# A spectral gate and a GEGLU layer, forward and backward: the inverse transform moves from pass one to pass two, in six classes of d mod 6

## The chip, the cores and the metric

One Trainium2 chip, one core of it. The time is device microseconds of one execution; lower is better. The engines are TensorE (PE, matmuls; PEld are its weight loads), VectorE (DVE), ScalarE (ACT), GpSimd (POOL) and SyncE (SP, which here issues most DMAs). Each engine executes its own instructions in the order in which the program lists them, and waits on semaphores for the others. In the profile, SPq and ACTq are the DMA issues in the instruction streams of SP and ACT.

## The reference

Two branches over x (2048 x 576, bf16) are mixed by a gate, and everything is differentiated by the gradient of the output:

```
g   = sigmoid((x * gate_w).sum(-1))                # one number per row
X   = rfft2(x) * (w_r + 1j * w_i)                  # 2048 x 289
a   = irfft2(X)                                    # spectral branch
b   = (gelu(B_x @ w_gate) * (B_x @ w_up)) @ w_down # F = 4608
out = g * a + (1 - g) * b
outputs: out, and the gradients to A_x, A_w_r, A_w_i, w_gate, w_up, w_down, gate_w
```

B_x enters as the same array x (`x = A_x` in the reference). The gradient to x through the spectral branch, dxa, is a second transform pair: the transform of the output's gradient (scaled by g), times the conjugate weights, transformed back. So there are two forward and two inverse 2-D transforms, of length S = 2048 along rows and D = 576 along columns.

## The kernel before

The kernel has a pass one and a pass two. The order of every engine's work is the order in which the Python code calls the instructions (a manual schedule); nothing reorders it.

**Pass one** walks over 18 groups g of 256 hidden columns, and in each over 4 pairs m of row blocks: 72 steps `pr`. A step makes the hidden activations and their gradients for 512 rows (`H_mm`, `H_act`, `H_ew1`, `H_ew2`), stores them to DRAM (`scr`), and executes the weight-gradient matmuls of the group before (`W_units`: dwd for w_down, dw for w_gate and w_up). Between these, `fft_next` drops the units of the transforms, spread evenly over the steps by `want(pr)`. In order: 32 + 32 forward units (`u1`, `u2`, along D and then the first part of S); table units (`tail_table`, `turned`); `mid` (`s2`: second part of the forward transform along S; products with the weights on DVE; `fold`; `s1`: first part of the inverse transform along S, stored to `scr_p1` and `scr_p2`); and at the end the inverse units of `inv_units`, once for a and once for dxa:

- `z(p)`: 8 matmuls of 128 columns (L888), the second part of the inverse along S for two of the 16 row classes, with the tables RT; evacuated by ACT, or by DVE in one place (L891);
- `ztail(p)`: 2 matmuls of 128 columns for the 68 columns left over (L901);
- `d(i)`: 6 matmuls for one row class (L915 with 145 columns, L917 with 290), the inverse along D; ACT or DVE evacuates (L923, L925), DVE adds and subtracts the halves (L926, L927), and SP stores the rows to `a_scr` or `dxa_scr`.

The halves come from `fold` (L810), which adds and subtracts the columns l and 288 - l before `s1`.

**Pass two** reads the stored activations back with transposing DMAs (`pin`, 144 of them, each 12 blocks of 128 x 128, six held ahead by `ensure`) and runs `jobs`: b (t) makes 128 rows of b with w_down; g (t) and u (t) make the two halves of the gradient to x with w_gate and w_up. One f0 step of a job is two `block`s of 12 matmuls of 288 columns (L1276), one for each half of the 576 columns. At jobs 1 to 9 `load_wuT` also loads a part of w_up, transposed. `post(t)` loads rows of a and of the output's gradient, and DVE makes the output and the gate's gradient; `x_end(t)` loads rows of dxa and finishes the gradient to x. PSUM has eight banks (`pacc`), handed out in pairs by `acc_pair`.

**Memory.** Two stacks of tiles grow from the two ends of the on-chip memory. `wstack` holds what pass one alone needs; it is closed before pass two's pools (p2f, p2bo, p2b, p2s, p2res) are opened, and these take the same addresses from the bottom up. A tile that lies where an earlier one lay waits for the last reader of that one. xn (all of x, 18,432 bytes in each partition) lies in `res`, which lasts to the end; dB is the first tile of `wstack`.

Of the kernel before, what the change touches and what calls it, by code (L numbers as in the profile page):

```python
# [10 lines left out]
ALU = mybir.AluOpType  # L11
# [14 lines left out]
D4NEW = 64  # L26
L2NEW = 95
# [13 lines left out]
HF = 145  # L41
QF = 73
NL = 2 * (HF - P)
# [21 lines left out]
def iotas(nc, res, unit):  # L65
# [9 lines left out]
    tb.lrow = unit([HF], F32, name="lrow")  # L75
    G.iota(tb.lrow[:], pattern=[[1, HF]], base=0, channel_multiplier=0, **kw)
    tb.dcol = res.tile([P, 8], F32, name="dcol")
# [3 lines left out]
    G.iota(tb.dcol[:, 5:7], pattern=[[1, 2]], base=0, channel_multiplier=2, **kw)  # L81
    G.iota(tb.dcol[:, 7:8], pattern=[[0, 1]], base=257, channel_multiplier=2, **kw)
    G.iota(tb.dcol[32:64, 7:8], pattern=[[0, 1]], base=256, channel_multiplier=2, **kw)
    tb.dn = res.tile([P, 8], F32, name="dn")
# [7 lines left out]
def iotas_R(nc, tb, res, unit):  # L92
# [12 lines left out]
    G.iota(tb.scol[:], pattern=[[1, T]], base=0, channel_multiplier=16, **kw)  # L105
    par_i = res.tile([P, 1], I32, name="par_i")
# [4 lines left out]
    def parity():  # L111
        V.tensor_single_scalar(par_i[:], tb.qcol_i[:], 1, op=ALU.bitwise_and)
        V.tensor_copy(tb.par[:, 1:2], par_i[:])
        V.tensor_scalar(tb.par[:, 0:1], tb.par[:, 1:2], -1.0, 1.0, op0=ALU.mult, op1=ALU.add)
        V.tensor_scalar(tb.kadd[:, 0, 1:2], tb.par[:, 1:2], float(S // 2), float(S // 4), op0=ALU.mult, op1=ALU.add)
        V.tensor_single_scalar(r4_i[:], tb.qcol_i[:], 3, op=ALU.bitwise_and)
        V.tensor_copy(tb.r4[:, 4:5], r4_i[:])
        for r in range(4):
            G.tensor_scalar(tb.r4[:, r:r + 1], tb.r4[:, 4:5], float(r), None, op0=ALU.is_equal)
# [8 lines left out]
def build_D(nc, tb, unit, c0, n, w):  # L128
# [11 lines left out]
    if c0 > 4:  # L140
        for c in range(n):
            G.tensor_scalar(X[:, c, :], tb.lrow[:, 0:w], tb.dcol[:, c0 + c:c0 + c + 1], None, op0=ALU.mult)
        G.tensor_tensor(X[:], X[:], y[:], op=ALU.add)

    def angles():
        for c in range(n if c0 <= 4 else 0):
            V.scalar_tensor_tensor(X[:, c, :], tb.lrow[:, 0:w], tb.dcol[:, c0 + c:c0 + c + 1], y[:, c, :],
                                   op0=ALU.mult, op1=ALU.add)
        V.scalar_tensor_tensor(y[:], X[:], -1.0, X[:], op0=ALU.mult, op1=ALU.max)

    def sines():
# [10 lines left out]
        elif c0 > 4:  # L162
            tb.Dt = [o[:, c] for c in range(n)]
# [10 lines left out]
    return angles, sines, tails  # L174

# [100 lines left out]
def kernel(  # L276
# [25 lines left out]
    a_scr = dram.tile([S, D], BF16, name="a_scr")  # L302
    dxa_scr = dram.tile([S, D], BF16, name="dxa_scr")
    scr_x = dram.tile([P, T, 2, DF], BF16, name="scr_x")
    scr_g = dram.tile([P, T, 2, DF], BF16, name="scr_g")
    scr_p1 = dram.tile([32, P, 2 * HF], BF16, name="scr_p1")
    scr_p2 = dram.tile([32, P, 2 * HF], BF16, name="scr_p2")

    xn = res.tile([P, T, D], BF16, name="xn")
# [5 lines left out]
    dOT = hres.tile([P, 5, T, P], BF16, name="dOT")  # L315
    dB = wstack.enter_context(tc.tile_pool(name="pdB", bufs=1)).tile([P, T, D], BF16, name="dB")
# [65 lines left out]
    tb.At2 = hres.tile([P, 2, 2, HF], BF16, name="At2")  # L382
    tb.Oi = hres.tile([P, 2, HF], BF16, name="Oi")
# [241 lines left out]
    def fwd_units(src, dst, scale, ps=pftile):  # L625
# [19 lines left out]
        def u2(t):  # L645
            def f():
# [13 lines left out]
                up = Vt[:, :, 0:2 * (HF - 1)].rearrange("p c (k l) -> p k c l", k=2)[:, :, :, 0:QF]  # L660
# [7 lines left out]
    def tail_table():  # L668

        n = HF - P  # L670
        nc.gpsimd.memset(tb.At2[:], 0.0)
        tp_ = pz.tile([P, 2, 1024], BF16, tag="z", name="tp")
        for k, r in ((2, P), (3, 32)):
            o = 512 * (k - 2)
            for c in range(2):
                nc.tensor.transpose(tp_[:, c, o:o + r], tb.Dt[k - 1][0:r, c, 0:P], ident[0:r, 0:r])
            for c in range(2):
                nc.tensor.transpose(tp_[0:n, c, o + 256:o + 256 + r], tb.Dt[k - 1][0:r, c, P:HF], ident[0:r, 0:r])
        nc.scalar.copy(tb.Oi[:, :, 0:P], tp_[:, :, 0:P])
        nc.scalar.copy(tb.Oi[:, :, P:HF], tp_[:, :, 512:512 + n])  # L680
        ot = unit([2, HF], name="ot")
        nc.scalar.copy(ot[0:n, :, 0:P], tp_[0:n, :, 256:256 + P])
        nc.scalar.copy(ot[0:n, :, P:HF], tp_[0:n, :, 768:768 + n])
        for c in range(2):
            for e, sb in enumerate((tb.Dt[2][32:64], ot)):
                r0 = 2 * n * c + (e ^ c)
                LD.dma_start(tb.At2[r0:r0 + 2 * n - 1:2, c, e, :], sb[0:n, c, :])

    tb.RT = []

    def turned(h):

        def f():
            tp_ = pftile(BF16)
            ts = range(8 * h, 8 * h + 8)
            for k, t in enumerate(ts):
                nc.tensor.transpose(tp_[:, 0, k * P:(k + 1) * P], tb.Rt[t], ident[:])
            if h == 1:
                for v in range(2):
                    nc.tensor.transpose(tp_[:, 1, v * P:(v + 1) * P], tb.B[:, v, :], ident[:])  # L700
            o = unit([8, P], name="RT")
            nc.scalar.copy(o[:].rearrange("p t m -> p (t m)"), tp_[:, 0, :])
            if h == 1:
                V.tensor_copy(tb.BT[:].rearrange("p v m -> p (v m)"), tp_[:, 1, 0:2 * P])
            tb.RT.extend(o[:, k, :] for k in range(8))
        f.room, f.last = 1.7, 2.0
        return f
# [12 lines left out]
    a_dv = a_scr[:].rearrange("(m i) d -> m i d", i=T)  # L720
    dxa_dv = dxa_scr[:].rearrange("(m i) d -> m i d", i=T)

    def mid_units():
# [40 lines left out]
        def products(p):  # L764
# [25 lines left out]
            def stack(k1, k2, conj, j):  # L790
# [9 lines left out]
                return f  # L800

            def fold(key):

                def f():
                    if key == "m1":
                        halve(st[p, "sm1"])
                    m = st[p, "s" + key][:].rearrange("p t j l -> p (t j) l")
                    q = unit([4, 2, HF], name="q" + key)
                    for e, op in enumerate((ALU.add, ALU.subtract)):
                        V.tensor_tensor(q[:, :, e, 0:HF - 1], m[:, :, 0:HF - 1], m[:, :, DF - 1:HF - 1:-1], op=op)  # L810
                    V.tensor_copy(q[:, :, :, HF - 1], m[:, :, HF - 1:HF].to_broadcast([P, 4, 2]))
                    st[p, key + "_q"] = q
                return f

            def out_dw():
# [8 lines left out]
                (0.9, lambda: (halve(G), mul("m1", X, W[:, 0])())), (0.8, mul("m2", X, W[:, 1])),  # L824
                (0.85, stack("m1", "m2", False, 0)), (0.85, stack("m1", "m2", False, 1)), (1.2, fold("m1")),
                (0.8, mul("n1", G, W[:, 0])), (0.8, mul("n2", G, W[:, 1])),
                (0.85, stack("n1", "n2", True, 0)), (0.85, stack("n1", "n2", True, 1)), (1.1, fold("n1")),
                (0.8, mul("o1", G, X[:, :, 0, :])), (0.8, mul("o2", G, X[:, :, 1, :])), (0.85, comb("o1", "o2", True)),
# [3 lines left out]
        def s1(p, key, b, dst):  # L832
            def f():
# [4 lines left out]
                q = st[p, key + "_q"][:].rearrange("p g e l -> p g (e l)")  # L838
                vps = pftile()
                for i in range(2):  # L840
                    nc.tensor.matmul(vps[:, i, :2 * HF], lhsT=tb.BT[:, int(p == 0 and b == 0 and i == 0), :], rhs=q[:, 2 * b + i, :],  # L841
                                     start=True, stop=True)
                Vt = half([2, 2 * HF], name="Vt")
                nc.scalar.copy(Vt[:].rearrange("p g (l e) -> p g e l", e=2), vps[:, :, :2 * HF].rearrange("p g (e l) -> p g e l", e=2))
# [20 lines left out]
    def inv_units(s, dv, scale):  # L865
        vp, zt = {}, {}

        def pre(i0):
            def f():
                Vp = vp[i0] = unit([2, 4 * HF], name="Vp")  # L870
                v = s[:].rearrange("g (k t c) l -> (g k) t c l", k=4, c=2)[:, i0:i0 + 2]
                LD.dma_start(Vp[:, :, 0:2 * HF], v[:, :, 0])
                LD.dma_start(Vp[:, :, 2 * HF + NL:], v[:, :, 1, 0:2 * P])
                LD.dma_start(Vp[:, :, 2 * HF:2 * HF + NL], v[:, :, 1, 2 * P:])
            f.noslot = True
            return f

        tails = {}

        def z(p):  # L880

            def f():
                Vp = vp[2 * p]
                zps = pftile()
                for ii in range(2):
                    for n in range(4):
                        c0 = (2 * HF + NL) * (n // 2) + n % 2
                        nc.tensor.matmul(zps[:, ii, n * P:(n + 1) * P], lhsT=Vp[:, ii, c0:c0 + 2 * P - 1:2],  # L888
                                         rhs=tb.RT[2 * p + ii], start=True, stop=True)
                zt[p] = unit([2, 4, P], name="ZT")  # L890
                pcopy[0](zt[p][:].rearrange("p i a m -> p i (a m)"), zps[:])  # L891
            f.wide, f.last = True, 2.0
            return f

# [531 lines left out]
```

## Time and profile before

| | us |
|---|---|
| median of three runs (lowest, highest) | 1379.36 (1379.34, 1379.62) |
| span of the profiled execution, first to last instruction | 1378.0 |
| first matmul of pass two | 949.80 |
| busy: PE, DVE, ACT, POOL | 1362.2, 789.5, 694.3, 261.9 |

The profile is one execution. Its page gives busy times, a picture of the span in 40 slices, and groups of instructions. DVE and ACT are busy in some seven to nine tenths of each slice of pass one, and in zero to six tenths of pass two:

```profile
DVE  7887777766989988876676766550002642121101
ACT  7887777767777877776766766651000000000000
```

Besides the page the trace answers questions: a timeline (start, duration, what), the list of waits (who waited for whom, in total), and busy times by stretch. A matmul's duration includes its way through the array, so matmuls that follow each other overlap in the timeline; the distance from start to start tells the rate.

### The profile page before, as it was taken

What the parts mean: (1) busy time and instruction counts of PE and PEld (TensorE: products, weight loads), DVE (VectorE), ACT (ScalarE), POOL (GpSimd) and SP (SyncE); (2) the same over time, 40 slices, a digit from 0 to 9 for tenths busy, and PEclk for the clock granted to TensorE, in tenths of its full rate; (3) what the DMA queues carried; (4) which work ended last, traced back from release to release, by engine and by line L of the source; (5) the groups of instructions that cost most, each with busy time, mean ns of one, the idle gap of its engine ahead of it and who ended that gap; (6) DMA issues with size and microseconds to landing.
All of it is one profiled execution on the core that took longest, in us unless ns stands there. A gap on an engine that the chain in (4) does not pass through costs nothing.

```text
span 1378.0 us, 25978 instructions
## 1 busy us (share of the span) xinstructions
PE 1362.2 (99%) x10186; PEld 909.0 (66%) x10272; DVE 789.5 (57%) x1526; ACT 694.3 (50%) x1288; POOL 261.9 (19%) x513
## 2 busy tenths in 40 slices
PE   9999999999999999999999999999999999999998
PEld 7566656556556556656656566556777777777776
DVE  7887777766989988876676766550002642121101
ACT  7887777767777877776766766651000000000000
POOL 6210111032444444331111011110000110000000
PEclk9999999999999999999999999999999999999999
DMA  7435444455566656555556666759999997878773
GB/s 234 126 92 150 113 124 128 129 161 154 131 163 158 169 155 168 145 144 145 144 146 163 164 163 153 180 127 280 198 192 201 218 191 169 157 161 166 156 150 88
DMA packets 512423, 218.95 MB, mean 159 GB/s; under 512 B 312010, under 2 KB 503180, under 8 KB 512300
## 3 DMA queue, kind: packets, MB, share of 16 engines
q1 hardware_dynamic: 495178, 191.89, 59.5%
q0 software_dynamic: 14912, 24.24, 6.4%
q8 instruction: 80, 1.31, 0.4%
q10 hardware_dynamic: 2210, 1.15, 0.3%
q14 instruction: 43, 0.35, 0.1%
HBM read 45.51 MB, written 98.30 MB: 104 GB/s over the span
## 4 chain that ended last, share of the span: by engine, by line
PE 96%; DVE 2%; issue 1%; DMA 1%; ACT 1%; ACTq 0%; SPq 0%; DVEq 0%
PE acc L1276 31%; PE wps L590 18%; PE xy L460 17%; PE wps L572 10%; PE z L444 9%; PE wps L604 2%; PE xy L453 2%; PE z L449 2%; PE pf L633 1%; PE pf L915 1%; PE pf L651 1%; PE pf L752 1%; PE pf L636 1%; PE pf L917 1%; PE pf L841 1%
## 5 line engine op out<-in xcount | busy, mean ns | idle before, releaser
L1276 PEld LDWEIGHTS <-pin 128*128 128x128 bf16 x3456 | 337.6, 98 | 86.2 <-issue 0.3
L590 PE MATMUL wps<-dH,xn 128*128 128x512 bf16 x1135 | 269.6, 379 | 1.0
L460 PE MATMUL xy<-wgu,xT 128*128 128x512 bf16 x1083 | 258.4, 380 | 8.3 <-issue 7.0
L460 PEld LDWEIGHTS <-xT 128*128 128x128 bf16 x1152 | 106.4, 98 | 132.6 <-issue 24.4
L590 PEld LDWEIGHTS <-xn 128*128 128x128 bf16 x1152 | 111.6, 98 | 119.0 <-issue 0.6
L1293 ACT COPY bo<-acc 128x288 f32<-128x288 f32 x32 | 12.8, 399 | 305.0 <-PE acc L1276 271.6
L572 PE MATMUL wps<-dB,A 128*128 128x288 bf16 x1152 | 153.8, 286 | 0.0
L597 POOL DMA_DIRECT2D out_dram<-dw x134 | 72.8, 547 | 402.5 <-ACT dw L541 366.9
L1276 PE MATMUL acc<-wgT,pin 128*128 128x288 bf16 x1152 | 143.8, 287 | 0.0
L1276 PE MATMUL acc<-wuT,pin 128*128 128x288 bf16 x1152 | 143.6, 287 | 0.0
L1276 PE MATMUL acc<-wd_all,pin 128*128 128x288 bf16 x1152 | 142.6, 287 | 0.0
L444 PE MATMUL z<-wdT,dOT 128*128 128x256 bf16 x1152 | 137.7, 273 | 0.1
L572 PEld LDWEIGHTS <-A 128*128 128x128 bf16 x1152 | 112.0, 98 | 32.9
L472 ACT ACTIVATE da<-z,omg 128x256 bf16<-128x256 f32 x288 | 112.1, 473 | 33.7 <-PE z L449 33.6
L444 PEld LDWEIGHTS <-dOT 128*128 128x128 bf16 x1152 | 112.3, 98 | 22.0 <-issue 0.9
L1348 DVE SCALAR_TENSOR_TENSOR f32t<-gwf,dlog,b16t 128x576 f32<-128x576 f32 x16 | 13.1, 817 | 173.6 <-DMA b16t<-dxa_scr 173.6
L481 ACT CAST xb<-xy 128x512 bf16<-128x512 f32 x144 | 85.0, 591 | 49.0 <-PE xy L460 49.0
L479 ACT ACTIVATE q<-xy 128x512 bf16<-128x512 f32 x144 | 88.1, 613 | 13.6 <-PE xy L460 12.4
L482 ACT CAST hu<-xy 128x512 bf16<-128x512 f32 x144 | 87.4, 607 | 0.0
L518 DVE TENSOR_TENSOR xb<-xb,sg 128x1024 bf16<-128x1024 bf16 x48 | 33.1, 691 | 79.8 <-ACT sg L510 79.7
L541 ACT CAST dw<-wps 128x512 bf16<-128x512 f32 x72 | 42.3, 589 | 53.3 <-PE wps L590 50.3
L1307 DVE SCALAR_TENSOR_TENSOR b16t<-b16t,g,f32t 128x576 bf16<-128x576 bf16 x16 | 13.1, 818 | 97.4 <-DMA b16t<-a_scr 97.1
(242 smaller groups left out, 1703.7 us busy)
## 6 DMA issues: line engine op xcount, KB each, us to landing
scr<-dH SPq DMA_DIRECT2D x144, 256.0 KB, 3.4
scr<-A SPq DMA_DIRECT2D x72, 256.0 KB, 2.5
out_dram<-dw POOLq DMA_DIRECT2D x134, 64.0 KB, 2.4
wd_all<-in_B_w_down_dram SPq DMA_DIRECT2D x3, 1728.0 KB
out_dram<-dwd POOLq DMA_DIRECT2D x34, 144.0 KB, 3.1
scr_p<-Vt SPq DMA_DIRECT2D x32, 145.0 KB, 3.0
wgu<-in_B_w_gate_dram SPq DMA_DIRECT2D x18, 256.0 KB, 5.1
wgu<-in_B_w_up_dram SPq DMA_DIRECT2D x18, 256.0 KB, 3.3
```

Source lines behind the costliest of these rows:

```text
L444: nc.tensor.matmul(zo(t), lhsT=dOT[:, ci, t, :], rhs=wdT[:, ci, :], start=(t % 4 < 2 and ci == 0), stop=False)
L460: nc.tensor.matmul(xy[k][:, t % 2, :], lhsT=xT[:, ci, t, :], rhs=wgu[:, ci, :], start=False, stop=(ci == 3))
L472: nc.scalar.activation(da[:, t, :], z[:, t % 2, t // 2, :], ACT.Copy, scale=omg32[:, 4 * m + t:4 * m + t + 1])
L479: nc.scalar.activation(q[:, h, :], xy[:, :, 0:FG], ACT.Square)
L481: nc.scalar.copy(xb[:, h, :], xy[:, :, 0:FG])
L482: nc.scalar.copy(hu[:, h, :], xy[:, :, FG:2 * FG])
L518: V.tensor_tensor(xb[:], xb[:], s[:], op=ALU.mult)
L541: wcopy[0](out, in_)
L572: nc.tensor.matmul(wps[:, :288], lhsT=tl(0, t)[:, fch * P:(fch + 1) * P], rhs=dB[:, t, h * 288:(h + 1) * 288], start=(t == 0), stop=(t == ...
L590: nc.tensor.matmul(wps[:].rearrange("p a b -> p (a b)"), lhsT=xn[:, t, c * P:(c + 1) * P], rhs=kt[t // 4][1][:, t % 4].rearrange("p k f -> ...
L597: wst[0].dma_start(ov[:, c, fsl], dw[:, k, :])
L1276: nc.tensor.matmul(acc[:, :288], lhsT=src[:, r, :], rhs=w_of(r)[:, h * 288:(h + 1) * 288], start=(first and r == 0), stop=(last and r == F ...
```

## The change

The inverse units leave pass one, and with them `fold`, `tail_table`, the D2 table, `a_scr` and `dxa_scr`. `s1` takes the product as it is (289 columns) and stores 289 columns. In pass two, the pool `sp` holds new tables and tiles; a and dxa are made there, 128 rows at a time, and stay on chip.

The transform along D is split by d mod 6: for each class r the 96 values of d = 6q + r need a sum over 49 folded columns of real and imaginary part, so 98 rows. DVE folds 578 values of a row class into 6 x 98 (`fold`, 17 instructions of 49 to 196 elements, fp32 and then bf16). `z_piece` multiplies the six parts with RT (6 matmuls, 98 weight columns, 128 columns each), ACT copies; `d_piece` multiplies with the table It (6 matmuls of 96 columns), ACT copies into the row order. RT and It are computed on chip at the start of pass two (`build_RT`, `build_I`); a small table `kc` for them goes through DRAM (`kscr`) at the start of the kernel to be turned.

A `piece(i, k)` is one z_piece (k = 0, 1) or d_piece (k = 2, 3) for a (even k) or dxa (odd k) of row class i, 64 in all. `tick`, called after a `block`, puts out the next piece when its count is due, every three or four blocks. `post` and `x_pre` take a and dxa from their tiles; `post` loads rows of x, since xn moves from `res` to be the first tile of `wstack`. The job list begins with two g jobs where it had three.

```diff
-    xn = res.tile([P, T, D], BF16, name="xn")
...
+    xn = wstack.enter_context(tc.tile_pool(name="pxn", bufs=1)).tile([P, T, D], BF16, name="xn")
     dB = wstack.enter_context(tc.tile_pool(name="pdB", bufs=1)).tile([P, T, D], BF16, name="dB")
...
-    fft = fg + [tail_table, turned(0), turned(1)] + mid[:-2] + pa + mid[-2:] + [gap] * 2 + ia[:-4] + pb + ia[-4:] + ib
+    fft = fg + [turned] + mid
...
-    jobs = [("g", t) for t in range(3)] + [("b", t) for t in range(8)] + [("u", t) for t in range(3)] + [("b", 8)]
+    jobs = [("g", t) for t in range(2)] + [("b", t) for t in range(8)] + [("u", t) for t in range(2)] + [("b", 8)]
...
+def build_RT(nc, tb, ftile, out):
+    w = ftile()
+    row, base, ts, off = w[:, 0:P], w[:, P:2 * P], w[:, 2 * P:2 * P + T], w[:, 2 * P + T:2 * P + 2 * T]
+    nc.gpsimd.iota(row, pattern=[[1, P]], base=0, channel_multiplier=0, **kw)
+    nc.gpsimd.iota(ts, pattern=[[1, T]], base=0, channel_multiplier=0, **kw)
+    V.tensor_scalar(base, row, tb.kc[:, 0:1], None, op0=ALU.mult)
+    V.tensor_scalar(off, ts, tb.kc[:, 1:2], tb.kc[:, 2:3], op0=ALU.mult, op1=ALU.add)
+    for t0 in range(0, T, 4):
+        X = ftile(I32)[:, 0:4 * P]
+        for t in range(4):
+            V.tensor_scalar(X[:, t * P:(t + 1) * P], base, off[:, t0 + t:t0 + t + 1], None, op0=ALU.add)
+        V.tensor_single_scalar(X, X, S - 1, op=ALU.bitwise_and)
+        nc.scalar.activation(out[:, t0:t0 + 4, :].rearrange("p t m -> p (t m)"), X, ACT.Sin, ...)
+def build_I(nc, tb, ftile, small, out):
+    X, y = ftile()[R], ftile()[R]
+    nc.gpsimd.iota(q_, pattern=[[0, 1]], base=0, channel_multiplier=1, **kw)
+    nc.gpsimd.iota(X.rearrange("p (r q) -> p r q", r=6), pattern=[[1, 6], [6, 96]], ...)
...
+    ts(X, X, mul, add)
+    ts(y, X, 1.0 / D, MAGIC)
+    ts(y, y, -MAGIC, -float(D), op0=ALU.add, op1=ALU.mult)
+    tt(X, X, y, ALU.add)
...
+    nc.scalar.activation(o, X, ACT.Sin, scale=2.0 * math.pi / D * EPS_SCALE)
+    V.tensor_scalar(o, o, half, None, op0=ALU.mult)
...
          tc.tile_pool(name="p2bo", bufs=8, **kw) as p2bo, \
-         tc.tile_pool(name="p2b", bufs=8, **kw) as p2b, \
+         tc.tile_pool(name="p2b", bufs=6, **kw) as p2b, \
+         tc.tile_pool(name="sp", bufs=1, **kw) as sp, \
...
+        build_RT(nc, tb, f32t, RT)
+        build_I(nc, tb, f32t, lambda shape: p2s.tile([P] + shape, F32, tag="icol", name="icol", bufs=1), It)
+        def load_p(i, w):
+            vp[i, w] = sp.tile([P, 2, DF], BF16, tag="Vp", name="Vp", bufs=4)
+            LD.dma_start(vp[i, w][:], srcs_v[w][:, i])
...
+        def z_piece(i, w):
+            F = ft.pop((i, w))
+            Z = zt[i, w] = sp.tile([P, 6, P], BF16, tag="Z", name="Z", bufs=2)
+            for b, ps in enumerate(acc_pair()):
+                for r in range(3):
+                    nc.tensor.matmul(ps[0:2 * LQ, r * P:(r + 1) * P], lhsT=F[:, 3 * b + r].rearrange("p c l -> p (c l)"),
+                                     rhs=RT[:, i, :], start=True, stop=True)
+                nc.scalar.copy(Z[0:2 * LQ, 3 * b:3 * b + 3].rearrange("p r m -> p (r m)"), ps[0:2 * LQ, 0:3 * P])
...
+        for i in range(2):
+            for w in range(2):
+                load_p(i, w)
+        for w in range(2):
+            fold(0, w)
+        ticks = [0, 0]
+        def tick(on):
+            ticks[0] += on
+            if pieces and ticks[0] >= ticks[1]:
+                pieces.pop(0)()
+                ticks[1] = ticks[0] + 3 + len(pieces) % 2
...
-            bo = bos[t] = p2bo.tile([P, D], F32, tag="bo", name="bo")
+            bo = bos[t] = p2bo.tile([P, D], BF16, tag="bo", name="bo")
...
                 for h in range(2):
                     block(accs[t][h], h, src, wT(k, f0), k == 1 and f0 == 0, k == 2 and f0 + FCB == NFC)
+                    tick(len(bos) + posted[0] > 0)
```

In `piece(i, k)`, after the matmuls, k = 0 and 1 issue the loads of row class i + 2, k = 1 and 2 emit the folds of i + 1, and k = 3 the `post`s that are due. In a b job `tick(1)` follows each block.

## The prediction

> **What bounds the kernel now.** I read the page's busy line first, then the list of what TensorE (PE) waited for.
>
> ```profile
> span 1378.0 us, 25978 instructions
> ...
> PE 1362.2 (99%) x10186; PEld 909.0 (66%) x10272; DVE 789.5 (57%) x1526; ACT 694.3 (50%) x1288; POOL 261.9 (19%) x513
> ```
>
> ```profile
> PE xy L460 <- issue: 7.0, 44, 0.2
> PE pf L944 <- POOL ident masks.py:199: 1.4, 1, 1.4
> ...
> PE pf L915 <- ACT ZT L891: 0.2, 1, 0.2
> PE pf L915 <- DVE ZT L891: 0.2, 1, 0.2
> ```
>
> Columns of the second: us in total, times, longest. PE waits for nothing that lasts. Whether it also runs at its rate is read from start times in PE's timeline (start us, us, what):
>
> ```profile
> 764.48 0.23 PE L915 MATMUL pf<-Dt,ZT 128*128 128x145 bf16 x1
> ...
> 764.99 1.89 PE L590 MATMUL wps<-dH,xn 128*128 128x512 bf16 x8
> 766.72 0.28 PE L901 MATMUL pf<-RT,Vp 128*68 128x128 bf16 x2
> 766.83 1.03 PE L590 MATMUL wps<-dH,xn 128*128 128x512 bf16 x4
> ...
> 781.48 0.61 PE L888 MATMUL pf<-RT,Vp 128*128 128x128 bf16 x8
> 781.92 2.12 PE L572 MATMUL wps<-dB,A 128*128 128x288 bf16 x16
> ...
> 949.80 8.98 PE L1276 MATMUL acc<-wgT,pin 128*128 128x288 bf16 x72
> ```
>
> From one start to the next: a z unit (8 matmuls of 128 columns) 0.44 us, 55 ns each; a d unit (6 matmuls, 764.48 to 764.99) 0.51; a ztail (2) 0.11. The last line is pass two's start: 72 matmuls of 288 columns in 8.9 us, 0.123 each. Neighbours follow at once, so both passes are sums of PE work. [...]
>
> **What comes off pass one.** z: 16 x 0.44 = 7.0. ztail: 16 x 0.11 = 1.8. d: 32 x 0.51 = 16.3. The transposes of tail_table (8) and of Rt (16) at 55 ns: 1.3. The two waits on ZT: 0.4. Together -26.8 us; 26.4 if the waits reappear elsewhere, 29.5 if joins that I don't see save some 3 us. DVE's fold (L810), d (L926, L927) and copies, and ACT's evacuations there, cost nothing now: PE's matmuls cover them, and the waits above show it. So does leaving out the D2 table at the start. The new kscr store and load hold SP for some landings (2 to 3 us) near 15 us; behind them stand the weight loads of g = 1, needed at 55 us.
>
> **What pass two gets on PE.** 64 pieces. z: 32 x 6 matmuls of 128 columns at 55 ns = 10.6. d: 192 matmuls of 96 columns; 128 columns take 55 ns, 145 take 63 to 65, so about 42: 8.0. Ends: 41 ns by columns alone, 55 if the weight load sets the pace. The narrower weights of z (98 columns) are nearest to L901's 68, whose matmuls also stood 55 ns apart. Together +18.6 (18.4 to 21.2). So the steady part is -8.2 us.
>
> **The first piece.** `tick` starts at ticks = [0, 0]. The first block of the first g job calls it with on = False: nothing is added, but 0 >= 0 holds, so piece (0, 0) is emitted there, 12 matmuls into pass two, not at the first b job. PE executes in order. That piece needs RT (build_RT) and the folded F of (0, 0), which stands on DVE behind all of build_RT and build_I. And these can't start early: xn has become the first tile of the stack that pass two reuses, 16 x 576 x 2 = 18,432 bytes, and p2f (4 x 2,304) with p2bo (8 x 1,152) is just that; the scratch of build_RT lies on xn, which the last dw matmul reads. That pass-two tiles wait for pass-one readers shows in DVE's timeline of before (in the bracket, what it waited for):
>
> ```profile
> 934.17 0.06 DVE L1252 MEMSET ones<- 128x1 bf16 x1 [8.11 <-DMA out_dram<-dwd]
> ```
>
> and ACT's timeline shows what stands ahead of the new sines:
>
> ```profile
> 950.00 0.58 ACT L541 CAST dw<-wps 128x512 bf16<-128x512 f32 x1 [2.87 <-PE wps L590]
> 953.26 1.02 ACTq L597 DMA_DIRECT2D out_dram<-dw  x2
> ```
>
> The last dw result is there at 950.0. ACT then holds until 954.3 for its last two stores, and build_RT's sines stand behind these. I take before's clock, in us:
> - POOL ramp 0.26 (L76), two DVE columns 0.2 each: 950.7.
> - Three groups of angles, each four tensor_scalars of 128 (0.217, L189) and one mask of 512 (0.427, L192): 1.3 each: 954.6.
> - The scratch ring has four tiles, so the fourth group waits for the first sine: 954.3 + table load 1.28 + 0.71 (L197) = 956.3; then 1.3: 957.6.
> - build_I: six columns at 0.15 (L208) 0.9; three operations on 576 at 0.516 (L1305), one at 0.752 (L1310): 960.8; sine about 0.8 (L158 took 0.667 for 435): 961.6; product 0.37 (L1044): 962.0.
> - fold: DVE took 0.305 for 146 fp32 elements (L658), 0.464 for 292 (L662); so 49, 98 and 196 elements cost about 0.20, 0.255 and 0.36. 4, 10 and 3 of them: 4.4 us: 966.4.
>
> PE arrives at 949.8 + 12 x 0.123 = 951.3. It stands still for 15.1 us. Behind the waiting matmul stand the other 60 of this g job, and SP's seventh pin, whose slot they free; six pins are already there, so nothing else comes late by it. Bounds: 12 if ACT's stores don't hold and a fifth of the DVE time overlaps; 18 if the 576-element ramp costs what L243's 128 did per element (0.874, so 3.9 us).
>
> After so long a pause the array is cold. At the start of this trace 128-column matmuls stood 107 ns apart from 1.38 us to about 6.4, 55 after: 5 us at half rate, 2.5 lost. I take 2.5; bounds 0 (no pause in mid-run is in this trace) and 3.4. [...]
>
> **What is hidden in pass two.** 32 folds at 4.4 = 141 us on DVE, which was busy 89 of 438 us there. A pair (8.8) and a post (some 4) are needed every 14 blocks, about 22 us, and each is emitted two or three pieces before its use; without that cover up to 4.4 us a piece would show. ACT gets 128 copies of 0.4: 51 of 438 us. The piece's two PSUM banks were copied a piece earlier. SP and the DMA engines are tighter. SP's timeline (start, us, what):
>
> ```profile
> 1025.49 3.49 SPq L1234 DMA_TRANSPOSE wuT<-in_B_w_up_dram  x1
> 1029.07 5.42 SPq L1201 DMA_TRANSPOSE pin<-scr  x3
> 1034.55 3.65 SPq L1234 DMA_TRANSPOSE wuT<-in_B_w_up_dram  x1
> 1038.29 11.16 SPq L1201 DMA_TRANSPOSE pin<-scr  x6
> ```
>
> A round of one wuT and three pins takes 9.06 us (1025.49 to 1034.55) against 8.84 of PE, with a DMA share above 1 in that stretch. After, each of the eight b jobs adds about 0.86 Vp load and 0.86 post load at 0.45 (L1301 and L1303 took 0.33 to 0.57; 0.8 us on SP) against 1.7 pieces at 0.29 (0.5 us) on PE: PE's lead shrinks by 0.5 us a job, 4 us. The pin of 1038.29 is used at about 1047.3 by count and lands in 4.3 to 6.1 us, so 1.6 us were spare. But while PE stands still the 5 MB of wd_all drain, which slowed pins 7 to 9 to 3.4, 3.1 and 2.6 us: some 4 us come back. I take 0; bounds 0 and 4. Pass two moves 48 loads of about 144 KB where it had 32 (L1301, L1346); the stores of a_scr and dxa_scr vanish from pass one.
>
> **Sum.** -26.8 + 18.6 + 15.1 + 2.5 = +9.4: span 1387.4. Median and span lie 1.4 apart (1379.36, 1378.0), so 1388.8 us.
>
> **Rivals.**
> 1. The first piece isn't held (scratch not on xn, or tables and fold ready by 951): 1379.4 - 8.2 = 1371.2. For it: the change does shorten PE's work, and two g jobs (17.8 us) stand ahead of the first b job. Against: the counter and the addresses above. Chance 0.07.
> 2. The hold is short: the chain overlaps better and the clock stays up. Hold and clock loss together below 11 us make no difference, below 5.4 a gain: about 1379. Against: some 13 us of DVE work alone lie in the chain. Chance 0.08.
> 3. The hold, and transposes that starve PE besides, by the SP rounds: 1392. For: 1.6 us spare; against: the drain. Chance 0.07.
> 4. My forecast, the hold alone: 0.78.
> That PE isn't the bound, and 26.8 us don't come back, I leave out: the start times exclude it.
>
> **Range and chances.** This kernel's measurement can't tell less than 0.2% (2.8 us). Slower by more: cases 3 and 4, 0.85. Same: case 2, 0.08. Faster: case 1, 0.07. Low end: -29.5 + 18.4 + 12 + 0 = +0.9, which needs every bound at once; I take +2.6, 1382. High: -26.4 + 21.2 + 18 + 3.4 = +16.2, 1395.6; 1395, which takes in most of case 3.
>
> **What would show it.** In the trace of after: a PE gap of 12 to 18 us after 12 matmuls of L1276's loop, ended by DVE's F; matmuls of 288 columns some 240 ns apart after it; pass two's start some 27 us earlier than 949.8; no L888, L901, L915, L917; other pieces without gaps. Wrong: no gap there (case 1), gaps on pin loads in the b jobs (case 3), or gaps at every piece, which would mean that fold isn't hidden.

## The result, and the profile after

The changed kernel takes 1388.6 us (median of four runs, 1388.0 to 1392.4) against 1379.4 us: 1.0068 times the time before, 95% interval 1.0054 to 1.0082. Five further runs beside others gave 1388.8 us and 1.0063 [1.0050, 1.0076].

The profiled execution is the slowest of the four runs, 1392.35 us with a span of 1390.6. The page's head:

```profile
span 1390.6 us, 26580 instructions
PE 1366.5 (98%) x10280; PEld 906.6 (65%) x10280; DVE 842.9 (61%) x1976; ACT 751.4 (54%) x1360; POOL 260.5 (19%) x508
PEclk9999999999999999999999999989999999999999
```

PE is nearly all of the span, as before, but one slice has lost clock, which no slice of before had. The list of PE's waits in the whole run (who waited for whom: us in total, times, longest):

```profile
PE acc L1244 <- DVE F L1235: 12.9, 1, 12.9
PE acc L1194 <- DVE b16t L1371: 4.4, 1, 4.4
...
PE acc L1244 <- DVE F L1236: 0.4, 1, 0.4
...
PE acc L1194 <- DMA pin<-scr: 0.3, 1, 0.3
```

Two waits make the list: the first z piece (L1244) for its folded tile F, 12.9 us, which was forecast, and a plain matmul of pass two (L1194) for DVE's L1371, 4.4 us, which was not. Their places in PE's timeline (start, us, what, in brackets what it waited for):

```profile
919.90 1.63 PE L1194 MATMUL acc<-wgT,pin 128*128 128x288 bf16 x12
934.44 0.34 PE L1244 MATMUL acc<-RTt,F 128*98 128x128 bf16 x1 [12.90 <-DVE F L1235]
935.23 0.77 PE L1244 MATMUL acc<-RTt,F 128*98 128x128 bf16 x5 [0.44 <-DVE F L1236]
935.79 8.81 PE L1194 MATMUL acc<-wgT,pin 128*128 128x288 bf16 x60
...
959.59 0.50 PE L1244 MATMUL acc<-RTt,F 128*98 128x128 bf16 x6
959.92 4.57 PE L1194 MATMUL acc<-wd_all,pin 128*128 128x288 bf16 x36
964.33 0.42 PE L1254 MATMUL acc<-It,Z 98*128 98x96 bf16 x6
...
1047.41 0.50 PE L1244 MATMUL acc<-RTt,F 128*98 128x128 bf16 x6
1052.36 7.26 PE L1194 MATMUL acc<-wd_all,pin 128*128 128x288 bf16 x36 [4.45 <-DVE b16t L1371]
```

Pass two begins at 919.90 where it began at 949.80, so 29.9 us are gone from pass one. Twelve matmuls later PE stands from 921.37 to 934.44. From then on a z piece takes 0.33 us of PE (959.59 to 959.92) and a d piece 0.26, and they fit between the others without gaps. At 1047.8 PE stands again. 36 matmuls after that wait take 7.26 us instead of 4.57, and the 60 after the first 8.81 instead of 7.5: half clock (0.50 granted). Windows of the same trace, with PE's busy time, granted clock, DMA share and GB/s:

```profile
924.80:934.40 9.60, 0.00 (x0) 0.50 0.54 168
934.40:938.40 4.00, 3.52 (x17) 0.50 0.14 37
938.50:945.00 6.50, 6.50 (x53) 1.00 0.89 124
1051.10:1057.90 6.80, 5.54 (x24) 0.50 1.05 195
```

In PE's records pass two lasts 424.7 us before (first matmul to last) and 467.1 after: +42.4. The parts: pieces 18.9 (192 matmuls at 55.8 ns and 192 at 42.8), hold 13.8, half clock after it 1.3 (11 matmuls 240 ns apart instead of 122.5), second wait 4.6 and its half clock 2.6 (22 matmuls), two late pins 0.7, unnamed 0.5. With the 29.9 off: +12.5 us; the spans differ by 12.6.

**Where the first hold comes from.** POOL's, ACT's and DVE's timelines:

```profile
920.19 0.24 POOL L213 IOTA f32t<- 128x128 f32 x1 [25.23 <-issue]
```

```profile
923.41 0.83 ACTq L643 DMA_DIRECT2D out_dram<-dw  x2
924.27 1.28 ACT L222 ACT_TABLE_LOAD   x1 [3.59 <-DMA wd_all<-in_B_w_down_dram]
```

```profile
926.32 0.87 DVE L220 TENSOR_SCALAR f32t<-f32t 128x128 int32<-128x128 f32 x4 [1.50 <-ACT RTt L222]
932.07 0.37 DVE L204 TENSOR_SCALAR It<-It,icol 98x576 bf16<-98x576 bf16 x1 [0.30 <-ACT It L203]
932.35 0.36 DVE L1221 TENSOR_TENSOR pm<-Vp 128x196 f32<-128x196 bf16 x1
935.09 0.36 DVE L1237 SCALAR_TENSOR_TENSOR F<-wp__11709 128x196 bf16<-128x196 f32 x1
```

The first instruction of the tables, POOL's ramp (L213), starts at 920.19, just after the last dw matmul has ended (914.50 + 5.56 = 920.06). That fits the scratch lying on xn, but the bracket names no releaser and no run here moves xn. ACT issues its last two stores from 923.4 to 924.2, after a wait that the profile puts down to a DMA, the table load follows, the fourth group of angles waits for the first sine (926.32), then come build_I until 932.4 and the fold until 935.4.

**Where the second wait comes from.** SP's and DVE's timelines around it:

```profile
1036.16 8.04 SPq L1120 DMA_TRANSPOSE pin<-scr  x4
1044.25 0.57 SPq L1319 DMA_DIRECT2D b16t<-in_A_x_dram  x1
1044.92 0.38 SPq L1321 DMA_DIRECT2D b16t<-in_grad_out_dram  x1
```

```profile
1049.14 0.76 DVE L1331 SCALAR_TENSOR_TENSOR f32t<-f32t,b16t 128x576 f32<-128x576 f32 x1 [15.07 <-DMA b16t<-in_grad_out_dram]
...
1051.84 0.82 DVE L1371 TENSOR_TENSOR b16t<-acc,f32t 128x288 bf16<-128x288 f32 x2
```

Four pins hold SP for 8 us; only then does it issue the loads of `post`. DVE idles 15.07 us for the second of them (L1331). Behind that instruction stands `x_end` (L1371), which empties two PSUM banks; the next b job needs them, and PE waits. A second profile (r1 below, span 1387.8) has the same two waits:

```profile
PE acc L1244 <- DVE F L1235: 12.8, 1, 12.8
PE acc L1194 <- DVE b16t L1371: 3.2, 1, 3.2
```

So the second wait belongs to the kernel; its size varies.

### The profile page after: what moved, and what is told of

Same layout as the page of the kernel before. It is cut to its first block, busy times and chain, and to the rows that moved or that the text cites. A ratio compares the mean times of both kernels' runs of the same rounds, so it can differ in the third digit from the quotient of the medians.

```text
span 1390.6 us, 26580 instructions
## 1 busy us (share of the span) xinstructions
PE 1366.5 (98%) x10280; PEld 906.6 (65%) x10280; DVE 842.9 (61%) x1976; ACT 751.4 (54%) x1360; POOL 260.5 (19%) x508
## 5 line engine op out<-in xcount | busy, mean ns | idle before, releaser
L1194 PEld LDWEIGHTS <-pin 128*128 128x128 bf16 x3456 | 336.5, 98 | 90.4 <-issue 5.4
L506 PE MATMUL xy<-wgu,xT 128*128 128x512 bf16 x1152 | 270.7, 380 | 0.0
L636 PE MATMUL wps<-dH,xn 128*128 128x512 bf16 x1152 | 265.6, 379 | 0.1
L1194 PE MATMUL acc<-wd_all,pin 128*128 128x288 bf16 x1152 | 149.2, 289 | 4.4 <-DVE b16t L1371 4.4
L618 PE MATMUL wps<-dB,A 128*128 128x288 bf16 x1152 | 149.6, 286 | 0.0
L1194 PE MATMUL acc<-wgT,pin 128*128 128x288 bf16 x1152 | 147.9, 287 | 0.0
L1194 PE MATMUL acc<-wuT,pin 128*128 128x288 bf16 x1152 | 146.6, 286 | 0.4 <-DMA pin<-scr 0.3
L1256 ACT ACTIVATE yo<-acc 128x288 bf16<-128x288 f32 x64 | 67.3, 1243 | 115.3 <-PE acc L1254 114.1
L1246 ACT CAST Z<-acc 98x384 bf16<-98x384 f32 x64 | 27.5, 482 | 129.6 <-PE acc L1244 129.6
L1331 DVE SCALAR_TENSOR_TENSOR f32t<-f32t,b16t 128x576 f32<-128x576 f32 x16 | 12.1, 759 | 119.5 <-DMA b16t<-in_grad_out_dram 119.5
L587 ACT CAST dw<-wps 128x512 bf16<-128x512 f32 x72 | 42.4, 590 | 66.9 <-PE wps L636 65.9
```

What stands on the lines that cost most here:

```text
L506: nc.tensor.matmul(xy[k][:, t % 2, :], lhsT=xT[:, ci, t, :], rhs=wgu[:, ci, :], start=False, stop=(ci == 3))
L587: wcopy[0](out, in_)
L618: nc.tensor.matmul(wps[:, :288], lhsT=tl(0, t)[:, fch * P:(fch + 1) * P], rhs=dB[:, t, h * 288:(h + 1) * 288], start=(t == 0), stop=(t == ...
L636: nc.tensor.matmul(wps[:].rearrange("p a b -> p (a b)"), lhsT=xn[:, t, c * P:(c + 1) * P], rhs=kt[t // 4][1][:, t % 4].rearrange("p k f -> ...
L1194: nc.tensor.matmul(acc[:, :288], lhsT=src[:, r, :], rhs=w_of(r)[:, h * 288:(h + 1) * 288], start=(first and r == 0), stop=(last and r == F ...
L1256: nc.scalar.activation(yv[:, 3 * b:3 * b + 3], ps[:, 0:288].rearrange("p (r q) -> p r q", r=3), ACT.Copy, scale=(SD2, 1.0)[w])
```

## The experiments

Ratios are to before, whose median lay between 1379.34 and 1379.46 us beside each run.

**e1: the first piece at the first b job**

```diff
-            if pieces and ticks[0] >= ticks[1]:
+            if on and pieces and ticks[0] >= ticks[1]:
```

> tick puts out a piece only when its argument is true, so the first piece stands in the first b job, 144 matmuls and more into pass two. My theory: the 12.9 + 0.4 us wait on F and the half-rate stretch after it (about 1.6 us) go away, so some 15 us less than the changed kernel: about 1374 us by the median, below before's 1379.4. Rival A: the tables and the first fold cost PE this time wherever the first piece stands; then the wait moves to the first b job and the time stays near 1388. Rival B: the hold gave SP and the DMA engines time to drain; without it pins and the loads of post come later still, and 3 to 5 us are given back as waits on pin or on DVE later: 1377 to 1379.

1377.4 us (1374.3 to 1379.2), 0.9983 [0.9975, 0.9992]. PE's waits in its profile (span 1377.4):

```profile
PE acc L1194 <- DMA pin<-scr: 3.4, 3, 1.4
PE acc L1244 <- DVE gwf L1186: 2.1, 1, 2.1
PE acc L1244 <- DVE b16t L1371: 2.0, 1, 2.0
```

The hold is gone, and 11.2 us with it (1388.6 to 1377.4), not the 15 expected: hold and half clock were worth that much, but other waits took some 4 back, as the expectation's rival B had it. Pins are late now, three times, as they were not with the hold, and the wait for L1371 is there as before. Besides, 2.1 us of the old chain are left. The first piece needs PSUM banks that DVE empties (L1186) only behind its tables and folds:

```profile
940.55 0.82 DVE L1186 COPY gwf<-acc 128x288 f32<-128x288 f32 x2
```

**e2: the first folds ahead of the tables**

```diff
-        build_RT(nc, tb, f32t, RT)
-        build_I(nc, tb, f32t, ..., It)
...
         for w in range(2):
             fold(0, w)
+        build_RT(nc, tb, f32t, RT)
+        build_I(nc, tb, f32t, ..., It)
```

> The first loads and the folds of row class 0 are emitted ahead of build_RT and build_I; nothing else moves. My theory: F was late because it stood behind these on DVE; now the first piece waits only for the first sine of RT, some 26 us of DVE and ACT order aside: in the changed kernel's profile that sine ended at 926.3, PE arrived at 921.4, so with two folds (6 us) ahead on DVE the first sine's angles are ready near 927 to 928 and PE waits 6 to 7.5 us in place of 13.3: 1381 to 1383 us. Rival: PE needs more of the tables than the first sine, or ACT's order sets the wait; then it stays at 12 us or more and the time near 1388.

1390.2 us (1386.2 to 1393.5), 1.0075 [1.0063, 1.0088]: a miss, no gain where some 6 us were expected. DVE's first fold instruction and PE's first piece:

```profile
927.86 0.36 DVE L1219 TENSOR_TENSOR pm<-Vp 128x196 f32<-128x196 bf16 x1 [19.41 <-issue]
```

```profile
936.54 0.80 PE L1242 MATMUL acc<-RTt,F 128*98 128x128 bf16 x6 [15.90 <-DVE f32t L220]
```

The fold couldn't start before 927.86: Vp is issued by SP from 917.2 on, behind the three loads of wd_all. Two folds (6.0 us) then stood ahead of the angles, which began at 933.88. In the changed kernel the tables cover Vp's way; taken apart, each is late by itself. That Vp's arrival set 927.86 is inferred from its issue; the bracket names no releaser.

**e3: post's two loads issued by POOL**

```diff
-            LD.dma_start(x_t[:], x_v[:, t, :])
+            ST.dma_start(x_t[:], x_v[:, t, :])
...
-            LD.dma_start(do_t[:], do_v[:, t, :])
+            ST.dma_start(do_t[:], do_v[:, t, :])
```

> The two loads of post are issued by POOL in place of SP; the first piece stays where it is. My theory: the second wait of PE (4.4 us on b16t of L1371, and half rate after it) comes from SP, which is late with its pins and wuT loads, so that DVE waits for the output gradient's rows and x_end behind it frees its PSUM banks late. With POOL's queue free the wait goes away: 4 us less by the median, 7 less where the profiled run had it: 1382 to 1385. Rival: the DMA engines themselves are full then, and the loads land late from any queue: no change, 1388.

1386.0 us (1384.5 to 1387.4), 1.0049 [1.0037, 1.0061], a little above the range expected. The second wait is gone from its profile; the hold is all that PE waits for in pass two:

```profile
PE acc L1244 <- DVE F L1235: 12.6, 1, 12.6
PE acc L1244 <- DVE F L1236: 0.4, 1, 0.4
```

**r1 and r2: the changed kernel and e3 again, side by side**

> The changed kernel again, beside r2 on one chip: four runs of it gave 1388.0 to 1392.4 us, and only the slowest was profiled. If the second wait of that profile (7 us with its half rate) belongs to the kernel, a second profile has it too or a pin wait of like size, and the median is 1387 to 1390 us. If it was a mishap of one run, PE has the hold alone and the run takes 1383 to 1386 us.

> e3_posts_pool again, on the same chip as r1: 1384 to 1387.5 us. If post's loads on SP cause the second wait, r1's median is 2 to 4 us higher; if not, the two are within 1 us.

r1 1388.8 us (1387.3 to 1390.0), r2 1385.8 (1383.6 to 1387.5), 1.0063 [1.0050, 1.0076] and 1.0038 [1.0024, 1.0052]. The medians lie 3.1 us apart, as expected of the cause named; the intervals just touch. Of all their runs, the nine of the changed kernel took 1387.3 to 1392.4 us, the ten of e3 and r2 1383.6 to 1387.5. r2's profile has a late pin (2.6 us) in place of the wait for L1371: the loads' place on SP made that wait, but not all lateness in pass two.

**e4: e1 and e3 together**

> Both edits: the first piece in the first b job, and post's loads on POOL. My theory: both waits go, and what is left is the steady part: before's 1379.4 less some 30 us of pass one plus some 19 us of pieces: 1368 to 1371. Rival: without the hold the pins come late (the DMA engines carry pins, wuT and the new loads at once), and PE waits for them some 3 to 5 us: 1372 to 1375.

1374.9 us (1373.2 to 1379.3), 0.9971 [0.9962, 0.9979]. The rival came true. One line is left:

```profile
PE acc L1194 <- DMA pin<-scr: 4.1, 2, 3.7
```

and the granted clock is at half from 988.3 to 995.1. What makes pins late without the hold? The next three runs ask whether it is the time that SP takes to issue, or the transfers.

**e5, e6, e7: taking loads off SP, on top of e4**

```diff
-        LD.dma_start_transpose(wuT[k]...)
+        nc.scalar.dma_start_transpose(wuT[k]...)
```

```diff
-            LD.dma_start(vp[i, w][:], srcs_v[w][:, i])
+            ST.dma_start(vp[i, w][:], srcs_v[w][:, i])
```

The first edit is e5, the second e6, both are e7.

> As e4_both, with the twelve transposing loads of wuT issued by ACT in place of SP. What is left in e4 is one late pin (a wait of 3.7 us at 989 us and the half rate after it, 2.8 us). Theory S, SP's issue is the bound: in e4 a round of SP is three pins of 1.8 us, one wuT of 3.2 to 6.1 us and 1 to 2 Vp of 0.55 us, 9.5 to 12 us against 9.5 us of PE; without wuT it is about 6.5 us, so no pin is late: 1367 to 1370 us, no wait for a pin. Theory D, the DMA engines are the bound (their busy share reads 1.05 to 1.37 in that stretch): the pins land as late as before whoever issues: 1372 to 1377 us with a wait for a pin. A third outcome: ACT stands 3 to 6 us in each issue and its PSUM copies come late, waits for ACT in place of DMA.

> As e4_both, with the Vp loads issued by POOL in place of SP. Theory S: SP gains 0.55 us for each piece that loads, some 0.9 us a round and 2.5 us for the four at the start (11.3 us in e4's trace), by 989 us about 8 us in all, more than the wait of 3.7 us: 1368 to 1371 us. Theory D: the same bytes move, so the pin at 989 us comes as late as before: 1373 to 1377 us.

> e5 and e6 together: SP issues pins and wd_all alone. Theory S: 1367 to 1369 us, no more than 1 us below the better of the two. Theory D: 1372 to 1377 us. If ACT's issues of wuT make its copies late, it is no better than e6.

e5: 1411.8 us (1409.6 to 1413.9), 1.0231 [1.0217, 1.0245]; e7: 1415.0, 1.0261 [1.0247, 1.0275]. Both lie far above every range expected. What SP waited for in e5 between 905 and 1100 us, and the three longest of PE's waits in its pass two:

```profile
SPq L1120 <- DMA wuT<-in_B_w_up_dram: 63.9, 9, 8.6
```

```profile
PE acc L1194 <- ACT yo L1256: 7.7, 1, 7.7
PE acc L1254 <- ACT Z L1246: 6.7, 2, 5.3
PE acc L1194 <- ACT Z L1246: 4.5, 1, 4.5
```

The pins on SP now wait for the wuT transposes on ACT, 63.9 us in nine waits; e4's list, with all transposes on SP, has no such wait. Why transposes on two queues wait for each other, no run shows. But the late pins are the smaller part of what PE lost: of its 30.8 us of waits 3.9 are for a pin and 26.9 for ACT. ACT's wuT issues come late in turn (one at 964.07, after ACT's copy of 949.31), which fits a wait for the pins, though the profile names no releaser; and ACT's PSUM copies stand behind them in program order (the next at 966.46, ACT idle 16.75 us before it). That is the third outcome named in e5's expectation, ACT's copies late, by a wait instead of a long issue (2.3 us each). These two runs therefore say nothing on SP's issue time.

e6: 1375.8 us (1372.1 to 1377.2), 0.9965 [0.9953, 0.9978], as e4. SP's timeline of e4 and of e6 (ends of eight rounds of one wuT and three pins):

```profile
935.25 3.65 SPq L1153 DMA_TRANSPOSE wuT<-in_B_w_up_dram  x1
938.98 6.23 SPq L1120 DMA_TRANSPOSE pin<-scr  x3
...
1019.93 4.13 SPq L1153 DMA_TRANSPOSE wuT<-in_B_w_up_dram  x1
```

```profile
932.27 3.22 SPq L1153 DMA_TRANSPOSE wuT<-in_B_w_up_dram  x1
935.59 7.86 SPq L1120 DMA_TRANSPOSE pin<-scr  x3
...
1017.30 3.63 SPq L1153 DMA_TRANSPOSE wuT<-in_B_w_up_dram  x1
```

84.7 and 85.0 us for eight rounds: 10.6 us each, with the Vp loads on SP or off it. The issues themselves got longer (three pins 7.9 us instead of 6.2 in the first round; over the eight rounds the transposes' rows of the timeline add up to 83.9 us instead of 78.8). PE needs some 9.5 us for a round, and it doesn't set SP's pace: counted from e6's PE timeline (24 matmuls a pin, six slots), the slot of the first pin of each round had been free for 3.9 to 13.7 us when SP issued it, an estimate. So the number of SP's issues isn't the limit; that what a round moves is, is the likelier reading.

**e8 and e9: pieces start four b jobs later**

```diff
-        ticks = [0, 0]
+        ticks = [0, 24]
```

e9 is the changed kernel with this alone; e8 has e4's edits besides.

> As e4_both, with the first piece four b jobs later (the count at which pieces start is 24 in place of 0). In e4 and e6 a round of three pins and one wuT took SP 10.6 us between 935 and 1020 us, with the Vp loads on SP or off it, against 9.5 us of PE, and the least issue times (1.4 us a pin, 2.6 us a wuT) would make 6.9: so the DMA engines set it, not SP's issue. Theory D: without the Vp loads and the loads and stores of post in the first four rounds (some 0.5 MB of 1.8 MB less), a round costs about 9 us, the lead of six pins lasts to the last wuT, and no pin is late: 1367 to 1371 us. Theory S (what counts is how many instructions SP issues, pieces or none): the lead is lost a few rounds later all the same, since the pieces that give SP time on PE (0.6 us a round) are gone too: 1373 to 1378 us with waits for pins near 985 to 1010 us.

> The changed kernel with that one number alone: pieces start at the count of 24, the loads of post stay on SP. The first z piece then stands behind some 54 us of other PE work, so the hold of 13.3 us and its cold clock are gone in any case. Theory D: 1367 to 1372 us. Theory S: a late load of post holds DVE and with it the PSUM banks as in the changed kernel, or pins are late: 1374 to 1380 us.

e8: 1369.9 us (1368.2 to 1370.8), 0.9933 [0.9919, 0.9946]. e9: 1371.1 us (1370.7 to 1371.3), 0.9940 [0.9927, 0.9952]. Both are faster than before and than the changed kernel; they don't differ by more than their intervals. PE's waits in pass two and its timeline, e9:

```profile
PE acc L1194 <- DMA wuT<-in_B_w_up_dram: 1.7, 1, 1.7
PE acc L1194 <- DMA pin<-scr: 0.3, 1, 0.3
```

```profile
919.91 8.98 PE L1194 MATMUL acc<-wgT,pin 128*128 128x288 bf16 x72
...
938.00 35.44 PE L1194 MATMUL acc<-wd_all,pin 128*128 128x288 bf16 x288
973.28 0.50 PE L1244 MATMUL acc<-RTt,F 128*98 128x128 bf16 x6
```

No gap up to the first piece at 973.28, and the clock stays full. e8's profile has one wait, 0.2 us, and a span of 1366.5: 1378.0 - 29.9 + 18.9 = 1367.0 is what pass one's saving and the pieces alone make. With no hold and no starving, the sum closes. Its first four rounds on SP, in which no piece loads, took 9.1 us each (934.94 to 971.26), e4's 10.3 (935.25 to 976.59).

## Why the prediction was right, and where it was not

The time forecast (1388.8) is the time measured (1388.6, again 1388.8), and the main cause was the one named. But the agreement to 0.2 us is luck: errors of both signs cancel. In r1's profile, which lies 0.7 us above its median:

| term | forecast | r1 |
|---|---|---|
| pass one | -26.8 | -30.0 |
| pieces on PE | +18.6 | +18.9 |
| hold of the first piece | +15.1 | +13.6 |
| half clock after it | +2.5 | +1.6 |
| SP and DMA late | 0 | +5.1 (3.4 and half clock 1.7) |
| unnamed | | +0.6 |
| sum | +9.4 | +9.8 |

- **Pass one: mis-sized, just beyond its top bound of 29.5.** From start to start over the whole pass, z and ztail took 9.3 us (8.8 forecast), d 17.2 (16.3), the transposes 1.8 (1.3); some 1.6 more came off neighbours that stayed (the dB and dH matmuls, some transposes). One unit read in mid-run left out its joins. The price of a unit is best summed over all its instances.
- **Pieces: right.** 55.8 and 42.8 ns against 55 and 42: here the columns (128 and 96) set the pace, not the weight load (98 weight columns in z, 128 in d). That PE's work is the bound is shown by e8, where all of what left pass one came through (span 1366.5, by the sum 1367.0).
- **The hold: right in place, cause and chain, mis-sized in one link.** Moved by the 29.9 us, the forecast chain had ACT's stores done at 924.4, the fourth angles at 926.4 and the last product ending at 932.1; the profile has 924.2, 926.3 and 932.4. The fold was put at 4.4 us and took 3.1: I added durations, but DVE instructions of 0.25 us that follow each other start 0.17 us apart here. And the first matmul needs only the part of F that L1235 writes (934.44); the other five start at 935.23. e1 and e9 show the hold by its absence.
- **Half clock: right in kind, 1.6 in place of 2.5**; half clock lasted 4.0 us from PE's resuming (4.6 in r1), not 5. No run shows the 3.4 us lost that the forecast's upper bound takes: after the hold 1.3 were lost in the changed kernel and 1.2 in e2 (60 matmuls in 8.75 us instead of 7.51), after e4's late pin some 2.8 (36 in 7.42 instead of 4.57). The clock went down 3.4 us after PE stopped at 921.37 in the changed kernel, some 3.9 us after the stop in r1, 2.9 in e4.
- **SP and DMA at 0: the step that failed.** "But while PE stands still the 5 MB of wd_all drain ... some 4 us come back" is half right: without the hold pins are late (e1 3.4 us, e4 4.1), with it hardly (0.3 us in the changed kernel, though once 2.6 in r2). But I asked only whether a pin is late for PE, and summed issue times. Pins also delay the loads behind them on SP (four pins 8.04 us), those hold DVE (15.07), DVE holds PSUM banks, and those hold PE (4.45). The do load had been costed at its 0.45 us of issue, with nobody named who waits behind the instruction that needs it; and this wait cost half clock on top (2.6 us). By form it is rival 3 in part: starved PE besides the hold, through another chain and for 5 us, 7 in the slowest run.
- **Rival 1's price came out, by luck too.** Without the hold 1371.2 were forecast; e9 has 1371.1. But pass one gave 3.1 us more than its term and the pieces cost 0.3 more, and 2.4 us of waits for a wuT and a pin, which had no term, took the difference back; e8, all but without waits, has 1369.9. It takes a later start of the pieces, not only the removal of the hold: e1 stops at 1377.4, with the loads of pieces and posts among those of wuT. That it is the transfers rather than SP's issues rests on e6's unchanged rounds; e8 and e9 agree, but they take loads and issues out of the early rounds together. Which part of the DMA path is full isn't settled.

## What to carry to other kernels

A piece of filler work that is emitted too early (here in the first g job instead of the first b job) stalls an engine that runs its work in order by its whole chain of producers (PE here by 12.9 us); look at the first call of the emitter with its counter at zero. Removing such a stall also removes the time in which loads caught up (waits for pins: 0.3 us with the hold, 3.4 in e1 without), so look at once at what else the DMA does there: putting the filler after the heaviest loads gave 17.5 us (1388.6 to 1371.1), removing the stall alone 11.2. When a queue is tight, follow who waits behind a late load through DVE and the PSUM banks, not only the tile that PE reads.

## What the runs showed of the hardware

- The half clock came in steps. In the changed kernel's trace the granted clock changes at 924.77, 938.42, 1051.06 and 1057.89, times that lie whole multiples of 3.41 us apart (4, 33 and 2); in e1 at about 1041.95 and 1045.36, worked out from its mean of 0.87 in 1039 to 1043 and 0.83 in 1043 to 1050. Half clock lasted about one such stretch there in e1, in e6 (mean clock of the run 0.999) and after r1's second wait (0.75 in 1050.5 to 1057.2), two (6.83 us) after the changed kernel's second wait and about as long in e4 (0.50 in 988.3 to 995.1), four (13.65) over the changed kernel's hold.
- So the length of a stop alone doesn't tell its price. In e1 half clock followed the 2.2 us from 1039.13 (at about 1041.95; 36 matmuls took 6.24 us instead of 4.57), but not the 2.2 us from 938.82 (48 took 6.04, as elsewhere). By steps of 3.413 us counted back from 1041.95, an estimate, the first stop lay within one stretch, and the second was divided at 939.55 into 0.7 and 1.5. Nor did r2's late pin, a wait of 2.6 us, cost clock: its mean over the run is 0.995, as in e3, which has the hold alone.
- In e6 the same transfer, a pin, took SP from 1.4 to 4.9 us to issue: an issue's length isn't a fixed price here. It grew as the Vp loads left SP's queue (78.8 to 83.9 us over eight rounds), which makes it a likely sign of the traffic.
- From run to run the variants spread by 0.6 us (e9) to 7.3 us (e2). e9's profile has 2.0 us of waits for loads in pass two; e8, whose profile shows the fewest waits (0.2 us), spreads by 2.6, so one profile doesn't tell the lateness of the other runs.
